# A hand-written order of tasks, rewritten from the eighth chunk on: the small product of B and C beside its neighbour's product of x and decays

## The chip, the cores and the metric

The kernel runs on one core of one Trainium2 chip. The metric is the device time of one execution in microseconds (us); the number compared is the median of several runs. Beside the runs there is one profiled execution, with a trace of every engine.

## What is computed

A scan over a sequence (a state-space layer in chunks), whose output goes through a small network that multiplies two projections:

```python
# attn: x (4, 8, 768, 32), a (4, 8, 768), B and C (4, 8, 768, 16)
cum = np.cumsum(log_a[chunk], axis=-1)
L = np.exp(cum[:, :, :, None] - cum[:, :, None, :]) * causal
CB = np.einsum('bhin,bhjn->bhij', Cc, Bc)
y_intra = np.einsum('bhij,bhjd->bhid', CB * L, xc)
y_inter = np.einsum('bhin,bhnd->bhid', Cc, state) * np.exp(cum)[..., None]
y[:, :, sl] = y_intra + y_inter
state = decay_full * state + sum_over_j(Bc * xc * decay_from_j)
# ffn: 3072 tokens, 256 -> 1024 -> 1024 -> 256
a = x @ w1; b = x @ w2
out = ((a * b) @ w3) @ w_out
```

## The kernel before

The sequence of 768 steps is cut into 16 chunks of 48 (c0 to c15). All work is written as small named tasks, and a string, PLAN, lists them in the order in which they are recorded. Each of the five queues (TensorE PE, VectorE DVE, ScalarE ACT, GpSimd POOL, and SP, which issues the DMAs) runs its own tasks in the order of that string and waits on semaphores for what another one makes. A word of the string is `task:engine@banks`: `c9.Z6:S` runs copy Z6 of chunk 9 on ACT (S; V is DVE, G is POOL), and `c9.MX@5,6` writes PSUM banks 5 and 6. For the tasks ending in `h` the number behind the @ is the slot in SBUF that holds the result. So the string fixes the order on every queue, the banks and slots, and who does each copy or sum.

The tasks of chunk c:

- `X`, `N`, `B`, `K`: loads by SP (x into `xe`, B into `bn` and `bc`, sums of logs into `ld` and `rd`). `X` fills a whole buffer `xe`, of which there are two, one for even and one for odd chunks.
- `D0`, `D1`: the exponents of the decays, one matmul each over 96 rows and 128 columns of the array (`ps<-rd,ld 96*128`). `E0`, `E1` take their exp on ACT. `W0`, `W1` (POOL) make the weighted B.
- `CB`: the product of B and C, 16 fp32 matmuls (32 records in the trace), each on 32 rows and 64 columns of the array (`ps<-bc 32*64`). `M0`, `M1` (DVE) multiply its two halves, which lie in two pairs of banks, by the decays.
- `MX`: x times the weighted decays and the old state, 32 fp32 matmuls (64 records) on 64 rows and 32 columns each (`ps<-r,xe 64*32`). It needs M, W and the state of the chunk before.
- `yi`: copies the output out of PSUM. `T` (DVE) transposes the state out of PSUM, `Z0` to `Z7` copy its eight pieces into the next chunk's `xe`, after the load `X` of that chunk. The next `MX` waits for all of them: MX, T, Z, MX is the chain from chunk to chunk.

The tasks of the network: `l<block>.<tile>.m` (two projections of a block of tokens), `a`, `g`, `h`, `l` (copy, product, rounding to fp32r and the rest); `d<block>.<tile>.m` adds one tile to the output (`ps<-fr,wo 128*128`, six matmuls), `y0`, `y1` transpose it out, `x` sends it out with 12 or 16 DMAs; `v`, `w`, `o` are weights; `s`, `x`, `q`, `t` do the last 1792 tokens with seven products in place of eight. All of these use the whole array (`128*128`).

```python
    def weigh(hf):
        w = R[:, hf * HG:(hf + 1) * HG, N:].rearrange("p (k g) s -> p k g s", k=2)
        tt("V", w, v["pc", hf], w, ALU.mult)
...
            def carry(e, q, z):
                i = z ^ (q & 1)
                copy(e, xn[64 * i:64 * i + N, q // 2, 4 * z:4 * z + 4], ZZ[32 * q:32 * q + N, 4 * z:4 * z + 4])
...
    for word in PLAN.split():
        name, _, banks = word.partition("@")
        name, _, engine = name.partition(":")
        b = [int(i) for i in banks.split(",")] if banks else []
...
            tasks.pop(name)(engine, b)
```

Of the kernel before, what the change touches and what calls it, by code (L numbers as in the profile page):

```python
# [24 lines left out]
k.act:S k.zero:V k.keep:G k.D1 t.D a.D +56x32n@0 +36x96@0 c0.B w0.D@0 k.R0:S k.L0:V t.clip:V c1.B a.clip:V t.ln:S c1.N a.ln:S c0.Y0:V k.D2 c0.N  # L25
c1.Y1:V +10x96@1 c1.X c0.Y1:V c0.X c1.Y0:V c0.D0@2 a.scan:V a.hi:V w0.L:V +10x96@3 c0.E0:S a.lo:G w0.A:S@0 c0.D1@4 w2.D@1 a.save w0.S:V c0.W0:G
c0.CB@5,6,0,1 c0.E1:S w0.H:V w1.D@2 k.S0:S c1.D1@7 c0.W1:G c0.M0:V c0.M1:V c1.D0@2 c1.E1:S w7.D@3 c2.K w0.P:V c1.W1:G c0.MX@3,4 c1.E0:S c1.W0:G
c1.CB@5,6,0,1 c0.T:V c2.X c1.M0:V c0.Z1:S c0.Z7:G +6@7 c0.Z3:S c0.Z6:G c0.Z2:S c1.M1:V c0.Z4:G c0.Z0:S c0.Z5:G c0.hi:S w6.D@0 w2.L:V w2.A:S@1 c0.lo:V
c1.MX@5,6 c1.hi:S w2.S:V c1.lo:V w2.H:S w2.P:V c1.T:V c1.Z6:G l0.0.m@1,3 c2.D1@2 c2.D0@0 w1.L:V w1.A:S@2 k.L1:S k.R1:S c2.N c1.Z2:S l0.2.m@4,7 w1.S:V
c1.Z3:S c2.B w4.D@1 c3.N c2.E0:S w7.A:S@3 w1.H:V w3.D@2 w1.P:V c2.E1:S c3.K l0.0.a:S w7.L:V l0.1.m@5,6 w6.A:S@4 w7.S:V c2.W1:G c1.Z0:S c1.Z4:S c3.X  # L30
w7.H:V l0.2.a:S c2.W0:G w5.D@3 w6.L:V w7.P:V c3.B l0.7.m@0,2 w6.S:V l0.1.a:S w6.H:S w4.A:S@0 v10.D@0 l0.0.g:V l0.1.g:V w6.P:V l0.2.g:V w4.L:V c1.Z7:S
c1.Z1:S l0.7.a:S w4.S:V c2.CB@3,4,5,6 w3.L:V l0.6.m@1,7 w4.H:S l0.7.g:V w3.A:S@1 w4.P:G c2.M1:V l0.6.a:S c2.M0:V c1.Z5:S w3.S:V c3.D0@2 c3.D1@0
c2.MX@3,4 c3.E1:S c4.K c3.E0:S c3.W1:G l0.4.m@1,5 c2.T:V c2.hi:S w5.L:V w3.H:S c5.N l0.6.g:V w5.A:S@2 o0.D@1 w3.P:G c2.lo:V c4.N l0.4.a:S w5.S:V c4.X
c2.Z0:S c3.CB@6,7,2,3 v10.A:S@3 v11.D@2 c2.Z6:G l0.3.m@0,4 c2.Z3:S c4.B c2.Z2:S c3.M1:V c2.Z4:S c3.W0:G w5.H:V c2.Z1:G l0.3.a:S c3.M0:V c2.Z7:G
c2.Z5:G l0.4.g:V c4.D1@1 c4.D0@2 w5.P:V c3.MX@5,6 c5.K l0.5.m@3,0 k.S1:S c3.hi:S c3.T:V v10.L:V c4.E1:S v13.D@3 l0.3.g:V c3.Z3:S c5.B c4.E0:S c3.lo:V
o0.A:S@4 c4.W0:G o0.L:V l1.5.m@7,1 c3.Z5:G l0.5.a:S v10.S:V c3.Z4:G l1.5.a:S l0.5.g:V o1.D@0 c4.W1:G v11.A:S@0 v11.L:V c3.Z2:G c5.D1@4 v10.H:S@0
c4.CB@5,6,2,3 c3.Z1:G c3.Z7:G c3.Z6:G l1.1.m@7,0 c4.M1:V o0.S:V l1.1.a:S v11.S:V v00.D@1 c6.B l1.5.g:V c5.D0@2 l1.4.m@3,7 c5.E0:S v12.D@2 c3.Z0:V
v13.L:V o0.H:S c5.X c4.M0:V c5.W0:G c6.K c5.E1:S o0.P:G v13.A:S@1 l1.7.m@1,2 v13.S:V v10.P:G l1.1.g:V l1.7.a:S l1.4.a:S v11.H:S@1 l1.4.g:V c4.MX@5,6
c5.W1:G l1.7.g:V v11.P:G c5.CB@0,1,3,4 c4.hi:S c6.X c4.T:V v00.A:S@2 c6.N l1.2.m@7,2 c5.M1:V v01.D@3 o1.A:S@4 v00.L:V c8.N o1.L:V v12.A:S@3 v12.L:V
v00.S:V c4.Z7:S l1.2.a:S l1.0.m@3,4 c4.lo:V c4.Z6:S v03.D@1 c4.Z4:S v13.H:S@2 c4.Z0:V c7.N l1.2.g:V o1.S:V v12.S:V c6.D0@7 c6.D1@5 c6.E0:S l1.3.m@6,2  # L40
c7.K c4.Z2:V c4.Z3:S c5.M0:V c6.W0:G l1.0.a:S c4.Z1:G c6.E1:S l1.0.g:V c4.Z5:G v00.H:S@3 c7.B c6.W1:G v13.P:V v02.D@0 l1.3.a:S c5.MX@0,1 v00.P:G
l1.3.g:V c6.CB@3,4,5,6 c5.hi:S c5.T:V c7.X v04.D@2 c5.lo:V v10.M@7,2 c5.Z6:G c6.M1:V c5.Z4:G c5.Z2:G c6.M0:V c5.Z0:G c7.D1@0 v03.L:V v12.H:S@0 c7.D0@1
v11.M o1.H:V c8.K c9.K v01.A:S@0 v01.L:V o1.P:V c5.Z5:S v03.A:S@1 l1.6.m@5,6 v12.P:V c5.Z1:V v01.S:V l1.6.a:S c5.Z3:S v02.L:V o3.D@3 c5.Z7:S v03.S:V
c7.E1:S v12.M c7.E0:S l1.6.g:V o2.D@1 v02.A:S@2 v04.L:V v01.H:V@1 c6.MX@3,4 v13.M c6.hi:S v04.A:S@4 c6.lo:V v02.S:V c6.yj:S v00.M@5,0 v04.S:V v14.D@0
c6.T:V v05.D@2 v01.P:V c6.Z5:S c6.Z4:G c8.B l2.2.m@1,6 v03.H:S@0 c6.Z0:V c6.Z6:G v02.H:S@2 o3.L:V v03.P:G o2.A:S@3 v02.P:V o3.A:S@0 l2.2.a:S c7.W0:G
v01.M v04.H:S@3 o3.S:V c6.Z7:G v14.A:S@1 o2.L:V v06.D@3 l2.5.m@3,4 c7.W1:G c8.X o2.S:V l2.2.g:V v17.D@1 v14.L:V v14.S:V l2.6.m@1,6 o2.H:V v14.H:S@1
v15.D@0 c6.Z2:V o2.P:V c10.N v05.A:S@2 c9.N v05.L:V o3.H:S c6.Z3:V c6.Z1:V l2.5.a:S o3.P:V v02.M l2.6.a:S v17.L:V v06.A:S@3 l2.6.g:V v17.A:S@0
l2.3.m@3,1 v04.P:V v17.S:V v15.A:S@4 l2.5.g:V l2.3.a:S v16.D@1 v17.H:V@2 v14.P:V v03.M v05.S:V v06.L:V v07.D@2 l2.3.g:V v14.M v05.H:S@0 v06.S:V
v16.A:S@1 v15.L:V l2.7.m@6,4 v06.H:S@1 v05.P:V v15.S:V v06.P:V v07.A:S@2 v07.L:V s0.a:V@3 v04.M v07.S:V v17.P:V v05.M v15.H:S@3 v16.L:V s0.c:G@0
l2.7.a:V v16.S:V pool.s v06.M l2.7.g:V v16.H:S@0 l2.0.m@3,1 v07.H:V@1 v16.P:V v07.P:V l2.0.a:S s0.b:V@1 s0.d:V@2 v07.M e00.a:S s0.1:V e01.a:S v15.P:V  # L50
s0.3:G l2.4.m@6,4 s0.S1h:S e00.b:V l0.0.h:S@1 e01.b:V l2.4.a:S l0.0.l:G s0.S1l:V v15.M s0.2:G l2.4.g:V l2.0.g:V c7.CB@5,6,3,4 l0.1.h:V@3 s0.S2h:S
s0.4:G c8.D0@0 c9.B c7.M1:V c8.D1@1 v16.M c8.E0:S c10.K c7.M0:V c8.E1:S s0.S2l:V c8.W0:G s0.S4h:S c8.CB@3,4,5,6 l0.2.h:S@0 c7.MX@0,1 l0.1.l:G c8.M0:V
c10.B d0.0.m@3,4 c7.yi:S c7.T:V c9.X s0.S4l:G c7.Z3:S c7.Z7:V c7.Z6:S c7.Z2:S c9.D1@0 c9.D0@1 c9.E1:S d0.1.m c11.K c7.Z5:G c7.Z4:V c9.E0:S c8.W1:G
c7.Z0:V c9.W1:G c8.M1:V l2.1.m@0,1 c9.W0:G c11.N l0.3.h:V@1 l0.4.h:S@3 c7.Z1:G c12.N l0.4.l:G l2.1.a:S s0.S3h:S l0.2.l:G s0.S3l:V c8.MX@5,6 l0.3.l:G
d0.2.m c8.yi:S c10.X l2.1.g:V c8.T:V d0.3.m l0.5.h:S@0 s1.a:V@4 c8.Z3:G c8.Z2:S c8.Z5:S c8.Z6:V c8.Z7:S c9.CB@0,1,5,6 c8.Z0:G s1.c:V@1 l0.6.h:S@1
c8.Z4:G c8.Z1:S v17.M c11.B c9.M0:V e10.a:S l0.6.l:G c9.M1:V e11.a:S e10.b:V c10.D1@0 c10.D0@1 c9.MX@5,6 l0.7.h:S@2 c12.K s1.b:V@0 c10.E1:S l0.7.l:G
# [4 lines left out]
c10.Z6:S c12.CB@0,1,5,6 l1.4.l:G l1.5.h:S@3 c10.Z3:V d0.x d1.2.m c10.Z0:S c10.Z4:S c10.Z7:S l1.5.l:G c12.M1:V d1.3.m c12.M0:V l1.6.h:S@0 s1.d:V@2
c11.MX@3,4 l1.7.h:S@1 l1.6.l:V s1.4:V l1.7.l:G d1.4.m c11.yi:S c11.T:V x0.B22h:S x0.B11l:V d1.5.m c11.Z5:S c11.Z6:S c11.Z7:G l2.0.h:S@2 c11.Z4:V
d1.6.m c11.Z0:G l2.0.l:V c11.Z1:G q0.0.P1@5 l2.1.h:V@3 l2.2.h:S@0 c11.Z3:G c13.X c11.Z2:V d1.7.m q0.0.s1:S@3 c14.B l2.1.l:V l2.2.l:V c13.D1@6
c12.MX@0,1 c13.E1:S l2.3.h:V@1 d1.y1:V c13.W1:G c13.D0@3 c12.yi:S c14.X d2.0.m@4,6 l2.3.l:G c12.T:V c13.E0:S c15.K d1.y0:V c12.Z4:S c12.Z6:S c12.Z3:V
c12.Z1:S c13.W0:G c13.CB@0,1,2,3 c12.Z5:V d1.x c12.Z7:G c13.M0:V d2.1.m c12.Z0:G c12.Z2:G c13.M1:V l2.4.h:V@2 s1.S3h:V d2.2.m l2.5.h:S@3 l2.4.l:V
s1.S3l:V c14.D1@7 l2.6.h:S@0 c13.MX@0,1 l2.5.l:V c14.E1:S l2.6.l:V c14.D0@2 c13.yi:S d2.3.m c14.W1:G c14.E0:S c13.T:V x0.B21h:V c13.Z6:S c13.Z1:G
c13.Z4:S c13.Z3:V c13.Z7:S c13.Z5:G c14.CB@0,1,2,3 c13.Z0:V l2.7.h:S@1 c13.Z2:G x0.B21l:V c14.W0:G d2.4.m c15.B c14.M1:V c14.M0:V d2.5.m l2.7.l:V
c15.X x0.T3:V@4 c14.MX@2,3 x0.B22l:V x0.T3h:V d2.6.m c14.yi:S x0.T1:V c14.T:V x0.T1h:S x0.T3l:V c15.D1@7 c14.Z7:G d2.7.m c14.Z3:S c14.Z0:S x0.T1l:V
# [787 lines left out]
```

## Time and profile before

| what | value |
|---|---|
| median of 3 runs | 264.86 us (264.73 to 265.08) |
| profiled execution | 264.53 us, span of its instructions 262.8 us |
| PE busy | 257.0 us (98%), 2870 matmul records |
| DVE, ACT, POOL busy | 205.2, 125.9, 113.2 us |
| granted TensorE clock | 1.00 |

The span runs from the first to the last instruction; the execution's own time has 1.7 us more around it. A matmul's row in the timeline gives its start and its length; matmuls overlap, so the distance from one start to the next, not the length, is what a matmul takes on PE. One row can stand for many matmuls of one kind (x12).

### The profile page before, as it was taken

Reading aid. Unit: us, or ns where it says so; the run is one execution under the profiler, and the core shown is the slowest. Engines: PE = TensorE matmul, PEld = TensorE weight load, DVE = VectorE, ACT = ScalarE, POOL = GpSimd, SP = SyncE. Lnnn points to the kernel's source line nnn. Section 1 sums busy time; section 2 is a strip of 40 time slices with the busy share of each in tenths; the row PEclk is TensorE's granted clock in tenths of the full one; section 3 lists DMA queues with packets and bytes.
Section 4 is the critical chain, followed back from the end, with each engine's and each line's share of the span. In section 5 each row is a group of like instructions: output and inputs, shape, how many; then the busy total and the mean of one; then the engine's idle time right before and its main releaser. Section 6 shows DMA issues by size and latency. Waiting matters only on the chain.

```text
span 262.8 us, 7259 instructions
## 1 busy us (share of the span) xinstructions
PE 257.0 (98%) x2870; PEld 224.9 (86%) x2870; DVE 205.2 (78%) x388; ACT 125.9 (48%) x270; POOL 113.2 (43%) x149
## 2 busy tenths in 40 slices
...
PEclk9999999999999999999999999999999999999999
...
GB/s 191 300 275 307 259 305 215 256 320 207 265 325 155 19 2 72 129 122 194 64 137 84 90 37 47 0 1 0 0 4 0 1 0 50 68 44 2 0 45 75
DMA packets 30009, 30.67 MB, mean 117 GB/s; under 512 B 15896, under 2 KB 22808, under 8 KB 29976
## 3 DMA queue, kind: packets, MB, share of 16 engines
...
q8 instruction: 22, 0.36, 0.6%
q14 instruction: 11, 0.09, 0.1%
...
## 4 chain that ended last, share of the span: by engine, by line
PE 92%; DVE 3%; issue 2%; DMA 1%; ACT 1%; DVEq 0%; ACTq 0%
PE ps L152 92%; DMA st<-in_w_dram 1%; DVE r L158 1%; DVE g L158 1%; DVE st L161 0%; DVE mag L441 0%; DVE wl L158 0%; ACT xe L164 0%; ACT mag L167 0%; DVE xT L158 0%; DVE z L363 0%; ACT r L167 0%; ACT xT L164 0%; ACT ob L164 0%; DVE zero L240 0%
## 5 line engine op out<-in xcount | busy, mean ns | idle before, releaser
L152 PE MATMUL ps<-xT,wh 128*128 128x384 f32 (+1 forms) x224 | 66.1, 363 | 0.6 <-ACT xT L164 0.6
L152 PE MATMUL ps<-fr,wo 128*128 128x384 f32 (+1 forms) x216 | 47.5, 365 | 0.0
L152 PEld LDWEIGHTS ps<-xT,wh 128*128 128x128 f32 x224 | 41.2, 188 | 5.0 <-ACT xT L164 0.7
L152 PEld LDWEIGHTS ps<-fr,wo 128*128 128x128 f32 x216 | 38.5, 188 | 4.6
L152 PE MATMUL ps<-xT,wl 128*128 128x384 f32 (+1 forms) x112 | 40.5, 362 | 0.0
L164 ACT COPY mag<-ps 128x384 f32<-128x384 f32 (+1 forms) x21 | 11.0, 526 | 35.8 <-PE ps L152 24.7
L158 POOL TENSOR_TENSOR r<-bn,r 128x128 f32<-128x128 f32 x32 | 15.8, 501 | 26.5 <-ACT r L167 9.7
L164 POOL COPY xe<-z 16x128 f32<-16x128 f32 x45 | 17.7, 393 | 21.2 <-DVE z L363 12.2
L152 PE MATMUL ps<-fr 128*128 128x256 f32 x192 | 25.2, 284 | 0.0
L152 PEld LDWEIGHTS ps<-fr 128*128 128x128 f32 x192 | 24.3, 191 | 0.8
L441 DVE SCALAR_TENSOR_TENSOR mag<-mag,st 128x512 uint32<-128x512 uint32 x28 | 21.5, 775 | 2.6 <-ACT mag L167 2.0
L158 DVE TENSOR_TENSOR mag<-ps,mag 128x384 f32<-128x384 f32 (+1 forms) x32 | 19.3, 616 | 4.6 <-PE ps L152 3.6
L152 PEld LDWEIGHTS ps<-xT,wl 128*128 128x128 f32 x112 | 21.1, 188 | 2.2 <-DVE wl L158 0.2
L164 ACT COPY g<-ps 128x384 f32<-128x384 f32 (+1 forms) x27 | 13.6, 507 | 16.6 <-PE ps L152 16.5
L167 ACT ACTIVATE mag<-st 128x512 f32<-128x512 f32 x28 | 18.7, 679 | 4.2 <-DMA st<-in_w3t_dram 2.6
L164 ACT CAST fr<-mag 128x512 fp32r<-128x512 f32 (+1 forms) x22 | 13.2, 610 | 15.0 <-PE ps L152 7.3
L158 DVE TENSOR_TENSOR r<-ps,r 128x384 f32<-128x384 f32 x32 | 16.7, 549 | 3.7 <-PE ps L152 2.2
L164 ACT COPY xe<-z 16x128 f32<-16x128 f32 x54 | 16.0, 296 | 5.4 <-DVE z L363 4.7
L158 POOL TENSOR_TENSOR fr<-mag,fr 128x512 fp32r<-128x512 f32 (+1 forms) x12 | 15.6, 1310 | 6.6 <-DVE fr L164 5.2
L167 ACT ACTIVATE r<-ps 128x384 f32<-128x384 f32 x32 | 14.9, 488 | 6.3 <-PE ps L152 6.0
L152 PE MATMUL ps<-xb,wh 128*128 128x384 f32 x64 | 16.3, 336 | 0.0
L152 PE MATMUL ps<-slot,wo 128*128 128x512 f32 (+1 forms) x72 | 15.9, 371 | 0.0
...
## 6 DMA issues: line engine op xcount, KB each, us to landing
...
```

Of the source, the lines that this page charges most:

```text
L152: pin(nc.tensor.matmul(*args, **kw))
L158: pin((nc.gpsimd if e == "G" else nc.vector).tensor_tensor(*args))
L164: pin(nc.scalar.copy(*args) if e == "S" else (nc.gpsimd if e == "G" else nc.vector).tensor_copy(*args))
L167: pin(nc.scalar.activation(*args, **kw))
L441: pin(nc.vector.scalar_tensor_tensor(m, m, 3, v["wl"].bitcast(U32), ALU.logical_shift_left, ALU.bitwise_or))
```

## The change

Only PLAN changes. It has the same 1167 words before and after: no task is added or removed. The orders on the five queues are the same up to the last matmuls of `l2.4.m`; from there the string is rewritten to its end. 152 tasks go to another engine. Banks and slots follow. Two lines of the string, of some 70:

```diff
-d0.4.m c10.E0:S c9.T:V c9.yi:S e11.b:V c11.X c9.Z7:S c10.CB@0,1,5,6 c10.W0:G x0.B11h:S l1.0.h:V@3 c10.W1:G c9.Z0:S c10.M0:V c12.B c9.Z6:S c11.D1@7
...
+c9.MX@6,7 c12.K l0.6.h:S@3 c10.W1:G c10.CB@4,5,2,3 c9.T:V l0.6.l:G c10.M0:V d0.5.m c9.Z0:S c12.B c9.yi:S c10.M1:V c11.X c9.Z4:S c9.Z2:G l0.7.h:S@1
...
```

From `c7.CB` to `c15.MX` there are nine CB and nine MX. Written in PE's order, with a bar wherever a matmul on the whole array stands between, they were `7CB | 8CB 7MX | 8MX | 9CB | 9MX | 10CB | 11CB | 10MX | 12CB | 11MX | 12MX | 13CB | 13MX | 14CB | 14MX | 15CB | 15MX` (17 groups) and are now `7CB | 8CB 7MX | 8MX | 9CB | 9MX 10CB | 11CB 10MX | 12CB 11MX | 12MX 13CB | 14CB 13MX | 15CB 14MX | 15MX` (11 groups).

PE, from `c9.MX` on. Names: `r,xe` is MX (odd chunks in `xe_96`), `bc` is CB (`bc_100` c10, `bc_101` c11), `rd,ld` the decays of c11 and then c12, `fr,wo` the tiles of `d0` and `d1`. Before:

```order
L152 MATMUL ps<-r_103,xe_96 32x64 x32
L152 MATMUL ps<-fr,wo 128x384 x6
L152 MATMUL ps<-bc_100 64x96 x16
L152 MATMUL ps<-rd_92,ld_90 128x384 x2
L152 MATMUL ps<-bc_101 64x96 x16
L152 MATMUL ps<-fr,wo 128x384 x6
L152 MATMUL ps<-r_102,xe_95 32x64 x32
L152 MATMUL ps<-rd_91,ld_89 128x384 x2
L152 MATMUL ps<-fr,wo 128x384 x24
```

Now, in the same place:

```order
L152 MATMUL ps<-r_103,xe_96 32x64 x32
L152 MATMUL ps<-bc_100 64x96 x16
L152 MATMUL ps<-fr,wo 128x384 x6
L152 MATMUL ps<-rd_92,ld_90 128x384 x2
L152 MATMUL ps<-fr,wo 128x384 x6
L152 MATMUL ps<-bc_101 64x96 x16
L152 MATMUL ps<-r_102,xe_95 32x64 x32
L152 MATMUL ps<-fr,wo 128x384 x6
L152 MATMUL ps<-rd_91,ld_89 128x384 x2
L152 MATMUL ps<-fr,wo 128x384 x12
L152 MATMUL ps<-bc_100 64x96 x16
L152 MATMUL ps<-r_103,xe_96 32x64 x32
```

The CB of c10 follows the MX of c9 at once, the CB of c11 no longer follows that of c10 behind two decays only, and between the MX of c10 and of c11 (the last row) stand three tiles of the network (18 matmuls), two decays and a CB.

ACT, from the exp of c12's decays to the copy `yi` of c11. Names: `r<-ps` is E, `fr` an `h` of the network, `xe_96` the Z of c10, `ya` a `yi`, `xT` a rounding of the last part. Before:

```order
L167 ACTIVATE r_102<-ps 128x8x48 x2
L164 CAST fr<-g_88 128x384 x2
L164 COPY xe_96<-z 16x4x32 x3
L164 CAST fr<-g_88 128x384
L164 COPY xe_96<-z 16x4x32 x3
L164 CAST fr<-g_88 128x384 x2
L164 COPY ya<-ps 128x2x192
```

Now, from the copy `yi` of c10 to that of c11:

```order
L164 COPY ya<-ps 128x2x192
L164 CAST fr<-g_88 128x384
L167 ACTIVATE r_102<-ps 128x8x48 x2
L164 CAST fr<-g_88 128x384
L164 COPY xe_96<-z 16x4x32 x3
L164 CAST xT_67<-ya 128x512
L164 COPY xe_96<-z 16x4x32
L164 CAST fr<-g_88 128x384
L164 COPY ya<-ps 128x2x192
```

The last Z of c10 on ACT stands behind both exps of c12, a rounding `fr`, three other Z and the rounding `xT`.

SP, around the output DMAs of block 0 (`out_dram<-g`, x12). Names: `xe_95` and `xe_96` are the x of c12, c13 and c14, `ld` and `rd` with 89 and 91 are the K of c14, `bn` are the N of c14 and c15, `bc_100` is the B of c14. Before:

```order
L155 DMA bc_101<-in_Ct_dram 128x640
L155 DMA bn_99<-in_Bn_dram 128x256
L155 DMA xe_95<-in_x_dram 128x512
L155 DMA ld_89<-cq 32x2x48
L155 DMA rd_91<-cq 2x16x48 x2
L155 DMA bn_97<-in_Bn_dram 128x256
L155 DMA out_dram<-g_65 32x4x64 x12
L155 DMA xe_96<-in_x_dram 128x512
L155 DMA bc_100<-in_Ct_dram 128x640
L155 DMA xe_95<-in_x_dram 128x512
```

Now:

```order
L155 DMA xe_95<-in_x_dram 128x512
L155 DMA bc_101<-in_Ct_dram 128x640
L155 DMA out_dram<-g_65 32x4x64 x12
L155 DMA bn_97<-in_Bn_dram 128x256
L155 DMA xe_96<-in_x_dram 128x512
L155 DMA ld_89<-cq 32x2x48
L155 DMA rd_91<-cq 2x16x48 x2
L155 DMA bn_99<-in_Bn_dram 128x256
L155 DMA bc_100<-in_Ct_dram 128x640
```

The K and the N of c14 and the N of c15 stand behind the twelve output DMAs now, as the x of c13 and the B of c14 did already.

## Rows read from the trace of the kernel before

**Rows 1.** The page: busy time and share of PE; its granted clock in 40 slices; the chain that ended last, by engine.

```profile
PE 257.0 (98%) x2870; PEld 224.9 (86%) x2870; DVE 205.2 (78%) x388; ACT 125.9 (48%) x270; POOL 113.2 (43%) x149
...
PEclk9999999999999999999999999999999999999999
...
PE 92%; DVE 3%; issue 2%; DMA 1%; ACT 1%; DVEq 0%; ACTq 0%
```

**Rows 2.** The chain that ended last, in order of time: start us, length us, what.

```profile
28.62 6.60 PE ps L152 x114
...
118.24 0.56 DVE r L158
...
120.69 138.59 PE ps L152 x1114
...
259.29 0.37 ACT ob L164
```

**Rows 3.** The view of waits, PE: who was waited for, us in total, times, longest.

```profile
PE ps L152 <- DVE r L158: 0.2, 1, 0.2
```

**Rows 4.** Timeline of PE in the last stage, where matmuls on the whole array follow one another: start us, length us, engine, line, operation, out<-in, rows*columns of the array, shape, count.

```profile
179.34 2.88 PE L152 MATMUL ps<-slot,wo 128*128 128x512 f32 x12
182.06 0.61 PE L152 MATMUL ps<-fr,wh 128*128 128x512 f32 x2
...
213.22 1.21 PE L152 MATMUL ps<-xb,ss 128*128 128x384 f32 x6
214.27 0.51 PE L152 MATMUL ps<-xb,wh 128*128 128x384 f32 x2
```

**Rows 5.** Timeline of PE from the decays of c8 to the MX of c10, same columns; in brackets idle time before, and what ended it.

```profile
100.63 0.62 PE L152 MATMUL ps<-rd,ld 96*128 96x384 f32 x2
101.08 1.60 PE L152 MATMUL ps<-fr 128*128 128x256 f32 x12
102.61 0.59 PE L152 MATMUL ps<-bc 32*64 32x96 f32 x32
103.13 0.86 PE L152 MATMUL ps<-r,xe 64*32 64x64 f32 x64
103.92 1.31 PE L152 MATMUL ps<-fr,wo 128*128 128x384 f32 x6
...
109.44 0.86 PE L152 MATMUL ps<-r,xe 64*32 64x64 f32 x64
110.22 2.38 PE L152 MATMUL ps<-fr,wo 128*128 128x384 f32 x12
112.53 0.59 PE L152 MATMUL ps<-bc 32*64 32x96 f32 x32
...
115.02 0.86 PE L152 MATMUL ps<-r,xe 64*32 64x64 f32 x64
115.80 1.34 PE L152 MATMUL ps<-fr,wo 128*128 128x384 f32 x6
117.07 0.59 PE L152 MATMUL ps<-bc 32*64 32x96 f32 x32
117.59 0.62 PE L152 MATMUL ps<-rd,ld 96*128 96x384 f32 x2
118.38 1.02 PE L152 MATMUL ps<-bc 32*64 32x96 f32 x32 [0.17 <-DVE r L158]
119.33 1.34 PE L152 MATMUL ps<-fr,wo 128*128 128x384 f32 x6
```

**Rows 6.** Timeline of PE, an MX with a CB directly behind it (c4 and c5), same columns.

```profile
47.77 0.86 PE L152 MATMUL ps<-r,xe 64*32 64x64 f32 x64
48.56 0.59 PE L152 MATMUL ps<-bc 32*64 32x96 f32 x32
49.08 0.44 PE L152 MATMUL ps<-xT,wh 128*128 128x384 f32 x1
```

**Rows 7.** Timeline of ACT, same columns: exp of decays, a `yi`, a rounding `h`, a rounding of 512 columns, three Z.

```profile
101.11 0.88 ACT L167 ACTIVATE r<-ps 128x384 f32<-128x384 f32 x2 [0.22 <-PE ps L152]
...
104.02 0.48 ACT L164 COPY ya<-ps 128x384 f32<-128x384 f32 x1 [1.13 <-PE ps L152]
...
113.24 0.52 ACT L164 CAST fr<-g 128x384 fp32r<-128x384 f32 x1
...
117.34 0.62 ACT L164 CAST xT<-ya 128x512 fp32r<-128x512 f32 x1
117.86 0.91 ACT L164 COPY xe<-z 16x128 f32<-16x128 f32 x3
```

**Rows 8.** Timeline of DVE, same columns: a T, the two M of a chunk, the two transposes `y0` and `y1` of a block of 384.

```profile
104.54 0.45 DVE L363 STREAM_TRANSPOSE z<-ps 128x256 f32<-128x256 f32 x1 [0.67 <-ACT ya L164]
...
117.77 1.02 DVE L158 TENSOR_TENSOR r<-ps,r 128x384 f32<-128x384 f32 x2 [0.18 <-PE ps L152]
...
250.15 1.10 DVE L565 STREAM_TRANSPOSE ob<-ps 128x384 f32<-128x384 f32 x2 [1.34 <-PE ps L152]
```

**Rows 9.** Timeline of SP: start and length of the issuing, per run of DMAs of one kind.

```profile
126.42 6.72 SPq L155 DMA_DIRECT2D out_dram<-g  x12
133.33 0.36 SPq L155 DMA_DIRECT2D xe<-in_x_dram  x1
...
137.62 6.11 SPq L155 DMA_DIRECT2D out_dram<-g  x12
```

More of the change, by code (lines that the diff above doesn't have):

```diff
@@ L24 @@
 PLAN = """
[L25 to L56, printed above, removed]
@@ L61 @@
[L61 to L68, printed above, removed]
```

98 lines of the change are left out of this document (69 added, 29 removed).

## The prediction

> **What bounds the kernel now.** I read the page first, then the chain that ended last, the waits of PE, and the timelines of PE, ACT, DVE and SP. PE is busy for 98% of the span, its clock is granted in full in every slice, and 92% of the last chain is PE [rows 1]. From 28.62 us on that chain never leaves PE but for one DVE step of 0.56 us at 118.24, and from 120.69 it is 138.59 us of PE in one piece, up to a last copy [rows 2]. The one DVE wait that the waits list for PE is that step [rows 3]. So from the place of the change on, the time is the sum of the distances between matmul starts, and a gain has to come out of that sum. The other engines matter only where PE would have to wait.
>
> Distances where only whole-array matmuls follow one another: (182.06 - 179.34) / 12 = 0.227 us for 512 columns, (214.27 - 213.22) / 6 = 0.175 for 384 [rows 4]. A CB takes 0.52 (102.61 to 103.13), an MX 0.79 (103.13 to 103.92) [rows 5].
>
> **The change part by part.**
>
> *Fewer changes of tile shape.* Between two products of small tiles, whole-array matmuls take longer than their distances say: from 110.22 to 112.53 twelve of 384 columns take 2.31, against 12 x 0.174 = 2.09, so 0.22 more; from 115.80 to 117.07 six take 1.27, against 1.05, again 0.22 [rows 5]. That price is paid per stretch between two small-tile groups, however long the stretch is. It is not paid between small tiles: the CB behind an MX starts 0.79 after it (47.77 to 48.56) and lasts 0.52 (to 49.08), the MX behind a CB lasts 0.79 [rows 5, 6], the lengths that they have alone. Whether decays stand apart or together costs nothing: a pair behind a CB takes 0.45 (100.63 to 101.08), 0.35 of it their distance and 0.1 the return from the CB, and what follows them goes on at its own distance, so they count as whole-array matmuls [rows 5]. The change takes 17 groups to 11, so six stretches vanish: 6 x 0.22 = **1.32 us**.
>
> [...]
>
> *The wait at 118 us.* Before, the CB of c11 writes the banks of the CB of c10 (0, 1, 5, 6) with two decays between, and has to wait for M0 and M1 of c10. The two decays from 117.59 last 0.79 in place of 0.35 + 0.22, the CB from 118.38 lasts 0.95 in place of 0.52, and the six matmuls from 119.33 (to the MX at 120.69) 1.36 in place of 1.27 [rows 2, 5]: 0.22 + 0.43 + 0.09 = **0.74 us**. Now d0.5, d0.6 and c11's decays stand between and the banks are others, so it goes.
>
> Without new waits the change would thus give 2.06 us.
>
> *New waits.* MX to MX is closer than before, so I walk the new order with these durations. Up to the MX of c8 (109.44) PE's rows are as before from 101.1 on. From there on each stretch is its matmuls' distances (0.174 for 384 columns, 0.227 for 512, 0.12 for 256 by the twelve from 101.08) plus 0.22, each CB 0.52, each MX 0.79. Without waits the MX of c9 then comes at 116.05, c10 at 120.5, c11 at 125.5, c12 at 131.0, c13 at 135.5.
>
> - *MX of c11.* It needs the last Z of c10 on ACT. D0 of c12 comes six matmuls after the MX of c10, at 120.5 + 0.79 + 0.11 + 6 x 0.174 = 122.45, and an exp starts 0.48 after its decay (100.63 to 101.11) [rows 5, 7]: 122.93. Then in ACT's order two exps (0.87), a rounding `h` (0.5), three Z (0.91), a rounding of 512 columns (0.52), the last Z (0.30) [rows 7]: 126.03. PE is there at 125.5: 0.55 late, or 0.35 if only the matmuls that read that piece wait (the eighth of 32 is the first). Bounds 0 (ACT's rows overlap by more) and 0.6; I take **0.45**.
> - *SP behind the outputs of d0.* They can start when `y0`, `y1` are done: d0.7 ends at 122.5, two transposes take 1.10 [rows 8], so 123.5. Twelve DMAs take 6.1 to 6.7 [rows 9], to 129.6 to 130.2; then come one load (about 0.45), the x of c13, and K of c14, issued by about 131.7. The nearest row for a landing is the end of the kernel: the last copy starts at 259.29 and lasts 0.37 [rows 2], and the span ends at 262.8, so about 3 us. An x issued at 130.4 lands near 133.4; the Z of c12, which write over it, could start at 132.9, and the MX of c13 has about half a microsecond to spare behind them. K would land near 134.7; the decays of c14 want it at 133.5 plus what was lost before (0.45). Bounds 0 (landing in 2 us) and 1.1; I take **0.3**, near the lower end, since the 3 us hold the hand-over from the last copy and the end of the program as well; that is a choice.
> - *Banks just freed.* D0 of c11 (bank 2) comes 0.1 before M1 of c10 ends: the M start 0.70 after their CB (117.07 to 117.77) and take 1.02 [rows 5, 8]; D1 of c14 is in the same position, behind the CB of c13. Bounds 0 and 0.3; I take **0.15**.
>
> Behind PE's own waits everything shifts together, and the order after `c15.MX` has the same matmuls. Walking it with the same durations I find DVE nearly full in the last 50 us but no product later than its bank. The outputs of block 2 go out much later than before, ahead of those of the last part; 16 DMAs at 0.51 (6.11 / 12) [rows 9] take 8 us there, which end before the next output is ready. Both at zero. If DVE's cover were gone, each evacuation of 384 columns would cost up to 0.55, the half of the row of two transposes [rows 8].
>
> *Sum.* -1.32 - 0.74 + 0.45 + 0.3 + 0.15 = -1.16 us. On the profiled execution: 264.53 - 1.16 = 263.4. The median of the runs lies 0.33 above it, so 264.86 - 1.16 = **263.7 us**.
>
> **The rivals.** (What a measurement of this kernel tells from no change is about 0.2%, 0.53 us.)
>
> 1. *No new waits.* The walk is too strict, ACT and SP are just in time. For it: the order before kept PE without any other wait from 28 us on [rows 2, 3]. 264.86 - 2.06 = 262.8.
> 2. *SP comes too late.* The upper bounds of the loads and of c11 hold, 1.1 + 0.6 + 0.3 = 2.0: 264.8, no change. For it: K moves behind twelve DMAs whose issue takes 6 us [rows 9]. Against it: in the old order, x issued at 133.33 behind the same DMAs [rows 9] held up nothing on PE.
> 3. *A joint costs as much as one change of shape.* Six pairs then keep half of 0.22 each and save 6 x 0.11 = 0.66: 264.86 - 0.66 - 0.74 + 0.9 = 264.4. Against it stand the rows at 48.56 and 103.13 [rows 5, 6]. That the change doesn't do what it says is this case.
> 4. *The chain MX, T, Z, MX becomes the bound: slower.* The shortest distance of two MX before is 115.02 - 109.44 = 5.58 us [rows 5]. The new order asks for 4.5 (c9 to c10), 5.0, 5.5, 4.5 (c12 to c13) and 4.4 (c14 to c15). If a chunk needed 5.58, these would fall short by 1.1 + 0.6 + 0.1 + 1.1 + 1.2 = 4.1, and the time would be 264.86 - 2.06 + 4.1 = 266.9. It decides from about 5.2 us per chunk on, where the shortfalls (0.7 + 0.2 + 0.7 + 0.8 = 2.4) pass the gain. Against it: MX to `yi` 0.89, `yi` 0.5, T 0.45, three Z 0.91 [rows 5, 7, 8] are 2.8 us; what fills the rest is other work in ACT's and DVE's queues.
>
> **How the numbers follow.** My forecast (net -0.6 to -1.7) 0.55; rival 1 0.20; rival 2 0.12; rival 3 0.05; rival 4 0.08. Faster than 264.33 are the forecast, rival 1 and half of rival 3: 0.78. Same: rival 2 and the rest of 3, 0.14. Slower: 0.08. The range reaches from rival 1 (262.8, a little below for its own spread) to rival 2 (264.8): 262.6 to 264.8. The likeliest case's own range is 263.2 to 264.3.
>
> **What would show it.** In the new timeline of PE the joined pairs start 0.79 or 0.52 after one another, and the stretch behind keeps its 0.22: then the first step holds. No wait before the CB of c11: the second. A CB or MX that lasts longer than 0.52 or 0.79, or a decay that does, marks a new wait; I look at the MX of c11 (ACT's Z), at the decays and CB of c14 (DMA), and at the Z of c12. The prediction is wrong if the joints cost 0.1 each, if the distance of two MX stays above 5 us where 4.5 is planned, or if PE waits after the MX of c15.

## The result, and the profile after

The changed kernel takes 266.87 us (median of 6 runs, 266.21 to 267.42), the kernel before beside it 264.80 (264.18 to 265.08): a ratio of 1.0079 (95% interval 1.0058 to 1.0100). It is 2.1 us **slower**; the forecast was 263.7 us, with a range of 262.6 to 264.8. The profiled execution takes 267.12 us with a span of 265.3, 2.6 more than the 264.53 of before.

The page of the changed kernel: busy time of PE, and the share of each engine in the chain that ended last [answers rows 1].

```profile
PE 257.3 (97%) x2869; PEld 225.2 (85%) x2870; DVE 204.0 (77%) x383; ACT 132.8 (50%) x287; POOL 103.3 (39%) x137
PE 80%; DMA 7%; DVE 4%; SPq 3%; issue 2%; ACT 2%; POOL 1%; DVEq 0%; POOLq 0%; ACTq 0%
```

PE does the same 257 us of work, but the last chain now leaves it for DMA, DVE, SP and ACT. The waits of PE say where: behind the start there was one of 0.2 us before [rows 3], now there are five.

```profile
PE ps L152 <- DMA bc<-in_Ct_dram: 1.4, 1, 1.4
...
PE ps L152 <- DVE g L565: 0.4, 1, 0.4
PE ps L152 <- ACT ya L164: 0.3, 1, 0.3
PE ps L152 <- DVE r L158: 0.2, 1, 0.2
PE ps L152 <- DVE xe L164: 0.2, 1, 0.2
```

The timeline of PE in order, to be read against [rows 5] (CB is `bc`, MX `r,xe`, decays `rd,ld`, `fr,wo` the tiles of d0 to d2):

```profile
104.12 1.31 PE L152 MATMUL ps<-fr,wo 128*128 128x384 f32 x6
105.68 0.62 PE L152 MATMUL ps<-rd,ld 96*128 96x384 f32 x2 [0.25 <-DVE r L158]
...
110.06 0.31 PE L152 MATMUL ps<-r,xe 64*32 64x64 f32 x6
110.62 0.81 PE L152 MATMUL ps<-r,xe 64*32 64x64 f32 x58 [0.25 <-DVE xe L164]
111.36 1.69 PE L152 MATMUL ps<-fr 128*128 128x256 f32 x12
112.89 2.25 PE L152 MATMUL ps<-fr,wo 128*128 128x384 f32 x12
115.41 0.59 PE L152 MATMUL ps<-bc 32*64 32x96 f32 x32 [0.27 <-ACT ya L164]
...
117.68 0.85 PE L152 MATMUL ps<-r,xe 64*32 64x64 f32 x64
118.46 0.59 PE L152 MATMUL ps<-bc 32*64 32x96 f32 x32
118.97 1.32 PE L152 MATMUL ps<-fr,wo 128*128 128x384 f32 x6
...
122.50 0.86 PE L152 MATMUL ps<-r,xe 64*32 64x64 f32 x64
123.29 1.33 PE L152 MATMUL ps<-fr,wo 128*128 128x384 f32 x6
124.46 0.51 PE L152 MATMUL ps<-rd,ld 96*128 96x384 f32 x2
125.34 2.35 PE L152 MATMUL ps<-fr,wo 128*128 128x384 f32 x12 [0.37 <-DVE g L565]
127.62 0.59 PE L152 MATMUL ps<-bc 32*64 32x96 f32 x32
128.14 0.86 PE L152 MATMUL ps<-r,xe 64*32 64x64 f32 x64
...
139.47 0.59 PE L152 MATMUL ps<-bc 32*64 32x96 f32 x32 [1.36 <-DMA bc<-in_Ct_dram]
```

Two things are as planned. The joined pairs cost only themselves (117.68 to 118.46 to 118.97: 0.78 and 0.51), so six stretches are gone, and the wait at 118 us is gone: 2.06 us less. What each stretch then takes beyond its matmuls and the usual 0.22 is the new part:

| where | beyond matmuls and 0.22, us | PE waits for |
|---|---|---|
| stretch from 104.12 | 0.57 (0.15 before) | a bank: decay of c9 behind M of c8, itself behind T of c7 |
| MX of c8, 110.06 | 0.51 | Z of c7 on DVE |
| stretch from 111.36 | 0.32 | `yi` of c8 on ACT (banks of CB of c9) |
| stretch from 115.93 | 0.15 | M of c9 (MX needs it, and the banks that it empties), behind two Z on DVE |
| stretches from 118.97, 128.93, pair at 121.87 | 0.25 + 0.21 + 0.11 | banks |
| stretch from 123.29 | 0.65 | `y0`, `y1` of d0: d1 takes its two banks |
| stretch from 135.17 | 1.65 | loads of c14 (1.40), a bank (0.25, which stays when the loads are early) |
| MX at 139.99, behind 152 us | 0.06 + 0.36 | small steps of 0.1 |

That is 4.7 us more than before, and -2.06 + 4.7 = +2.6, the difference of the two profiled executions. Two small things that this sum leaves out nearly cancel: PE comes to this part 0.2 us later than before (104.12 against 103.92), and a stretch of the old order (from 148.06) took some 0.1 too much as well.

Two causes can be read at once. SP issues the loads of c14 behind the 12 DMAs of d0.x; that of its `bc`, the load B, begins at 134.36:

```profile
125.37 6.40 SPq L155 DMA_DIRECT2D out_dram<-g  x12
131.87 0.38 SPq L155 DMA_DIRECT2D bn<-in_Bn_dram  x1
...
134.36 0.43 SPq L155 DMA_DIRECT2D bc<-in_Ct_dram  x1
```

And two small Z on DVE, usually 0.22 us each (the median of 13 from 100 to 156 us, in either trace), take 1.60 together, then a cast that takes 0.42 in the trace of before (at 139.59) takes 1.40:

```profile
108.96 1.60 DVE L164 COPY xe<-z 16x128 f32<-16x128 f32 x2
110.59 1.40 DVE L164 CAST wh<-mag 128x512 fp32r<-128x512 f32 x1
...
114.95 1.58 DVE L164 COPY xe<-z 16x128 f32<-16x128 f32 x2
```

Over the same time POOL runs s1.b and s1.c, two additions of 1.25 us, and beside the two Z from 114.95, which stand ahead of M of c9, it runs s1.1, a third addition that was on DVE before:

```profile
109.20 2.51 POOL L158 TENSOR_TENSOR mag<-wh,wl 128x512 f32<-128x512 f32 x2
...
115.17 1.27 POOL L158 TENSOR_TENSOR mag<-mag,mag 128x512 f32<-128x512 f32 x1
```

The second Z ends at 110.57 and the cast at 111.99, the first two additions at about 110.5 and 111.7. The chain that ended last has that Z, and the load of c14 from its issue to its landing:

```profile
109.33 1.24 DVE xe L164
...
134.36 4.98 DMA bc<-in_Ct_dram
```

### The profile page after: what moved, and what is told of

It reads as the page before. It is cut to its first block, busy times and chain, and to the rows that moved or that the text cites. A ratio compares the mean times of both kernels' runs of the same rounds, so it can differ in the third digit from the quotient of the medians.

```text
span 265.3 us, 7235 instructions
## 1 busy us (share of the span) xinstructions
PE 257.3 (97%) x2869; PEld 225.2 (85%) x2870; DVE 204.0 (77%) x383; ACT 132.8 (50%) x287; POOL 103.3 (39%) x137
## 4 chain that ended last, share of the span: by engine, by line
PE 80%; DMA 7%; DVE 4%; SPq 3%; issue 2%; ACT 2%; POOL 1%; DVEq 0%; POOLq 0%; ACTq 0%
PE ps L152 80%; SPq L155 3%; DMA bc<-in_Ct_dram 3%; DMA bc<-in_c_dram 2%; DMA cq<-cp 1%; DVE z L363 1%; ACT ya L164 1%; DVE xe L164 1%; ACT xe L164 1%; DVE r L158 1%; DVE st L161 1%; DVE g L158 1%; ACT fr L164 0%; POOL fr L158 0%; DVE mag L441 0%
## 5 line engine op out<-in xcount | busy, mean ns | idle before, releaser
L152 PE MATMUL ps<-fr,wo 128*128 128x384 f32 (+1 forms) x222 | 49.2, 364 | 0.4 <-DVE g L565 0.4
L152 PEld LDWEIGHTS ps<-fr,wo 128*128 128x128 f32 x222 | 39.6, 188 | 5.0 <-DVE g L565 0.7
L158 POOL TENSOR_TENSOR r<-bn,r 128x128 f32<-128x128 f32 x32 | 16.5, 521 | 27.0 <-ACT r L167 16.8
L164 POOL COPY xe<-z 16x128 f32<-16x128 f32 x42 | 15.8, 376 | 24.1 <-DVE z L363 13.7
L158 DVE TENSOR_TENSOR mag<-ps,mag 128x384 f32<-128x384 f32 (+1 forms) x29 | 17.4, 611 | 8.9 <-PE ps L152 6.3
L164 ACT CAST fr<-mag 128x512 fp32r<-128x512 f32 (+1 forms) x21 | 12.5, 598 | 19.5 <-DVE mag L158 7.9
L164 ACT COPY xe<-z 16x128 f32<-16x128 f32 x57 | 16.9, 296 | 8.2 <-DVE z L363 7.0
L164 ACT COPY tmp<-ps 128x512 f32<-128x512 f32 (+1 forms) x17 | 9.2, 550 | 22.6 <-PE ps L152 13.4
```

Source lines behind the costliest of these rows:

```text
L152: pin(nc.tensor.matmul(*args, **kw))
L158: pin((nc.gpsimd if e == "G" else nc.vector).tensor_tensor(*args))
L164: pin(nc.scalar.copy(*args) if e == "S" else (nc.gpsimd if e == "G" else nc.vector).tensor_copy(*args))
```

## The experiments

Each was timed beside the kernel before, whose medians were 264.76 to 264.96. The stage meant below runs from the CB of c7 to the end of the MX of c15; its length is worked out from PE's timeline (53.70 us in the changed kernel). 27 matmuls of 512 columns that lie inside it in the old order lie behind it in the new one, so only lengths of one order are compared. Diffs show words of PLAN; `...` marks what is left out.

### Parts of the change alone, on the kernel before

**e3: only the wait at 118 us.**

```diff
-c11.CB@0,1,5,6 ... d0.5.m
+d0.5.m c11.CB@0,1,5,6 ...
```

> The kernel before with the one tile d0.5 moved between the decays and the CB of c11 (and its rounding l0.5.l ahead of l1.0.h on DVE). Theory: the wait of 0.74 us at 118 us, CB of c11 for banks that the CB of c10 still holds, goes without the joining of groups, since another 1.04 us of matmuls stands there: 264.1 us against 264.8. Rival: the wait moves to the next MX or tile, because M1 of c10 sets the time there and not the banks alone: 264.8.

264.22 us, 0.9976 (0.9964 to 0.9989): 0.7 less, as expected. PE of e3, in the place of the last three of [rows 5]:

```profile
118.14 1.22 PE L152 MATMUL ps<-fr,wo 128*128 128x384 f32 x6
119.28 0.66 PE L152 MATMUL ps<-bc 32*64 32x96 f32 x32
119.88 1.32 PE L152 MATMUL ps<-fr,wo 128*128 128x384 f32 x6
```

The CB takes 0.60 in place of 0.95, and the decays ahead of it wait no more. The second term holds, and it needed no joined pair.

**e4: only one pair joined.**

```diff
-c12.CB@0,1,5,6 ... c12.M1:V ... c12.M0:V ... c11.MX@3,4 ... c11.T:V
+c12.CB@0,1,5,6 c11.MX@3,4 ... c11.T:V c12.M1:V c12.M0:V
```

> The kernel before with one group joined: the CB of c12 directly ahead of the MX of c11, M1 and M0 of c12 behind the T of c11. Theory (a stretch of matmuls on the whole array between two small groups costs 0.22 us beyond its matmuls, and joining saves that once, with nothing new to wait for): 264.6 us against 264.8, and in the trace 0.79 + 0.52 us for the pair with no gap between. Rival (joining brings a wait of its own, as M of c12 comes later on DVE): 264.9 to 265.3.

264.94 us, 1.0001 (0.9988 to 1.0013): a gain of 0.2 us lies inside the interval, and so does no gain. The trace shows the gain: from the CB of c7 to the end of the MX of c15 it takes 56.13 us against 56.32, 0.19 less, with the pair standing as forecast:

```profile
128.68 0.59 PE L152 MATMUL ps<-bc 32*64 32x96 f32 x32
129.19 0.86 PE L152 MATMUL ps<-r,xe 64*32 64x64 f32 x64
129.98 1.31 PE L152 MATMUL ps<-fr,wo 128*128 128x384 f32 x6
```

The profiled execution reached the CB of c7 0.43 us later than that of before, in a part that the edit does not touch; against such differences a gain of 0.2 is not to be seen in a time.

**e8: both.** 

> The kernel before with both single edits: d0.5 between the decays and the CB of c11, and the CB of c12 directly ahead of the MX of c11. Theory (the two are 8 us apart and add, 0.7 and 0.2 us): 264.0 us against 264.9, and both gaps closed in the trace. Rival (the M of c12 behind the T of c11 come too late now that PE is 0.7 us earlier): 264.2 to 264.5.

264.20 us, 0.9963 (0.9951 to 0.9975). It is faster than both kernels and as fast as e3. Its stage takes 55.75 us, e3's 55.67, so the second gain does not add: 0.13 us goes in the stretch from 129.44 (0.37 beyond its matmuls, 0.24 in e3), the rest in steps under 0.1, some ahead of both edits.

### The loads behind d0.x

**e1: d0.x behind the loads.** Block 1's output gets its own room, since it would otherwise wait for d0.x.

```diff
-... d0.x d1.0.m ... c15.X d1.y1:V ... d1.x
+... d1.0.m ... c15.X d1.y1:V ... d0.x d1.x
-outs(f"d{sl}.", ..., lambda: G0[:, :1024])
+outs(f"d{sl}.", ..., lambda: G1[:, :1024] if sl == 1 else G0[:, :1024])
```

> The changed kernel with one thing taken away: block 1's transposed output gets a room of its own in SBUF, and the 12 DMAs of d0.x are issued on SP behind the load X of c15 in place of ahead of the loads of c13 to c15. Theory 1 (the loads are late because SP issues 12 output DMAs first): the wait of 1.36 us of the CB of c14 for bc, 1.65 with its stretch, is gone, so about 265.3 us against 266.9 for the change; d1.x comes later and costs nothing. Rival (the load lands late whatever stands ahead of it, or the time is given back at the next MX, which waits for the Z of the chunk before): 266.5 to 267.0.

268.81 us, 1.0161 (1.0132 to 1.0189): slower still. The stage takes 52.34 us, 1.36 less, so the first half of theory 1 holds; but the part behind 152 us takes 111.3 in place of 109.3. ACT shows why:

```profile
154.75 0.62 ACT L164 CAST ss<-mag 128x512 fp32r<-128x512 f32 x1 [3.17 <-DMA out_dram<-g]
```

The last part's buffers take G1's place, and wait for the late d1.x that still reads from it. That is a fault of the room chosen, not of the order.

**e5 and e11: another room** (`YB` of the last part begins at G0's word 1536, block 1's output is in words 768 to 1535). **e10** has the room alone; **e12** and **e13** are single profiled executions of e5's kernel.

> As the run before with d0.x behind c15.X, but the room for block 1's transposed output is now in the buffer of block 0's products (768 words of it, the last part's second x moved up by 512 words), not in one that is given to the last part's buffers at 152 us. Theory (the first room made those buffers wait for the late d1.x, which cost 2.0 us behind 152 us, and the load of c14 is late by SP alone): no wait for the load, no wait behind 152 us, 265.5 us against 266.9 for the change. Rival (the late d1.x holds up something else, or the 1.4 us are given back at a later wait): 266.5 or more.

> The control of the run with the second room: the changed kernel with block 1's transposed output in the buffer of block 0's products and the last part's second x moved up by 512 words, but with d0.x where the change has it. Theory 1 (a place in SBUF costs nothing): as the change, 266.9 us. Theory 2 (the place costs something, by which the run with d0.x behind c15.X lost what it gained): 267.4 or more.

> The run with the second room and d0.x behind c15.X once more, beside its control on the same chip. Theory 1 (the load of c14 is worth the 1.4 us that its stage shows, and the profiled execution started late by chance): 0.9 to 1.4 us under the control. Theory 2 (most of it is lost again): 0.3 us under the control, or nothing.

> One more profiled execution of the kernel with the second room and d0.x behind c15.X, to see where an execution of 266.5 us loses what one of 265.5 us does not. Theory 1: in the loads and decays ahead of 27 us, as in the first of its profiled executions. Theory 2: behind 152 us. Theory 3: at a wait between 100 and 152 us that the two profiled ones do not show.

> A third look at the same kernel, with the same three theories: the loss ahead of 27 us, between 100 and 152 us, or behind 152 us.

| run | time, us | profiled | to the CB of c7 | stage | rest to the last matmul |
|---|---|---|---|---|---|
| the change | 266.87 | 267.12 | 98.87 | 53.70 | 109.30 |
| e10, room alone | 266.41 | 266.53 | 98.56 | 53.43 | 109.30 |
| e5 | 266.56 | 266.64 | 99.67 | 52.29 | 109.46 |
| e11 | 266.60 | 265.51 | 98.48 | 52.33 | 109.47 |
| e12 | one execution | 265.73 | 98.69 | 52.35 | 109.47 |
| e13 | one execution | 266.21 | 98.91 | 52.60 | 109.49 |

In all four traces with d0.x behind the loads the stage is 1.1 to 1.4 us shorter than in the change, and PE has no wait for a DMA there. In e11 SP issues the load at 130.89, and on PE (second view) the CB of c14 follows its decay without a wait:

```profile
130.89 0.43 SPq L155 DMA_DIRECT2D bc<-in_Ct_dram  x1
```

```profile
137.40 0.34 PE L152 MATMUL ps<-rd,ld 96*128 96x384 f32 x1
137.70 0.59 PE L152 MATMUL ps<-bc 32*64 32x96 f32 x32
```

0.16 to 0.19 is given back behind 152 us. The medians show less: e5 and e11 lie 0.3 under the change, and not under e10, the control of e11, which shows that the new room alone costs nothing. Part of what is missing is the time to the CB of c7, which the edit does not touch and which ranges from 98.48 to 99.67. Of the theories on where an execution loses it, the first fits e5, which comes 0.8 us later than the change to the CB of c7. e12 and e13 lost little anywhere (0.25 in one stretch of e13) and were short, so they do not show what a long execution loses. How much of the 1.1 to 1.4 us a run without a trace gains stays open.

**e14: the 12 DMAs left out. e15: 20 in place of 12.**

```diff
-for g in range(NR4):
+for g in range(0 if n == "d0." else NR4):              # e14
+for g in [0, 1, 2, 0, 1] if n == "d0." else range(NR4): # e15
```

> The changed kernel without the 12 DMAs that send block 0's output out (d0.x; that part of the output is left out). Nothing else moves. Theory 1 (these 12 stand ahead of the loads of c14 on SP, and the wait of the CB of c14 costs 1.1 to 1.4 us in an ordinary execution): 265.4 to 265.8 us against 266.4 to 266.9, and no wait of PE for a DMA behind 100 us. Theory 2 (what the load costs in its stage is given back at a later wait, whatever takes it away): 266.4 or more, with a new wait of PE behind 140 us. Theory 3 (no new wait, but executions without the 12 DMAs start late as often): the median near 266.5 and single executions at 265.5.

> The changed kernel with 20 DMAs in place of 12 in d0.x: two of its three groups of rows are sent out twice, the same data to the same place. SP is held 8 x 0.53 = 4.2 us longer at that place. Theory 1 (in ordinary executions the loads behind d0.x already hold up PE, as in the profiled one): the whole 4.2 us come on top, 270.7 to 271.1 us. Theory 2 (in ordinary executions the loads have some slack, and only the profiled ones were late): 4.2 less that slack, 269.5 to 270.2 for a slack of about 1 us. Theory 3 (the loads' place on SP doesn't matter): 266.9.

e14: 266.11 us (265.46 to 267.05). Its stage takes 52.37 us, with no wait for a DMA and no new one of size; the profiled execution came late, at 99.76, to the CB of c7. The median is 0.8 under the change, between theory 1 (265.4 to 265.8) and theory 3 (near 266.5); no new wait and a late start are what theory 3 says.

e15: 271.91 us (271.31 to 273.40), 5.0 over the change where its 8 more DMAs hold SP 4.1 us longer (10.48 in place of 6.40). SP, then PE, then the view of a window, whose columns behind the five engines are the granted clock, the share of the DMA engines and GB/s:

```profile
126.31 10.48 SPq L155 DMA_DIRECT2D out_dram<-g  x20
```

```profile
141.17 0.42 PE L152 MATMUL ps<-rd,ld 96*128 96x384 f32 x1 [3.67 <-DMA rd<-cq]
143.40 0.94 PE L152 MATMUL ps<-bc 32*64 32x96 f32 x32
```

```profile
142.00:145.00 3.00, 3.00 (x90) 2.34 (x93) 1.64 (x4) 2.23 (x6) 1.11 (x3) 0.50 0.68 210
```

The decay of c14 waits 3.67 us for K. Behind that wait the granted clock is 0.50 from 142 to 145 us, and from this decay to the end of the MX of c13 PE needs 4.19 us (141.17 to 145.36), against 3.04 in e14 (137.35 to 140.39): 1.15 more, taken here as the slower clock's. The stage is 3.5 us longer than in the change: about 3.67 + 1.15, less the change's 1.40. The place of the loads on SP matters, so theory 3 falls. Theories 1 and 2 are not told apart: all six runs have a mean clock of 0.985 to 0.994 (0.998 to 1.00 in the change), and what they would take at the full clock is not known.

How long an ordinary execution of the change waits for these loads therefore stays open. Worked out as the 1.40 was, the profiled executions of e10 and of e2 (below), with d0.x in the same place, lose 1.14 and 0.6. The load B itself is not always equally long: from issue to landing it takes 4.98 us in the change, 5.23 in e6, 4.08 in e9 and 3.77 in e10, under 3.4 in e2 (issued at 134.87, used at 138.21 without a wait) and under 3.8 in e15 (139.69, 143.40). So it is late by its place behind d0.x and by a long transfer together; what makes the transfer long was not followed.

### Copies on DVE beside POOL, and `yi`

**e2: s1.b and s1.c on DVE.**

```diff
-s1.b:G@4 ... s1.c:G@2
+s1.b:V@4 s1.c:V@2
```

> The changed kernel with the two sums s1.b and s1.c on DVE instead of POOL. Theory 1 (a small copy from SBUF to SBUF on DVE stands still while POOL adds, so that the Z of c7 and c8 on DVE end 1 us late): the DVE copies of 109 to 115 us take 0.2 instead of 1.2 us, the MX of c8 does not wait in its middle (0.51 us) and the CB of c9 does not wait (0.3 us), so 0.5 to 0.8 us less than the change, about 266.2 us. Rival (DVE is full there, and 1 us more of sums on it holds up T and M): 266.9 to 267.5, with waits of PE for DVE where the others were. A third outcome: the copies on DVE are as slow without POOL beside them, and then nothing of the 0.8 us goes.

DVE of e2, the same two Z and the same cast:

```profile
108.91 0.58 DVE L164 COPY xe<-z 16x128 f32<-16x128 f32 x2
109.88 0.43 DVE L164 CAST wh<-mag 128x512 fp32r<-128x512 f32 x1 [0.39 <-PE ps L152]
```

0.58 in place of 1.60 and 0.43 in place of 1.40: the third outcome falls, and the cause is shown. The two Z beside s1.1, which stays on POOL, take 1.58 us here too. The MX of c8 takes 0.79 again. But the kernel takes 267.13 us, 1.0071 (1.0045 to 1.0098), no less. At 134.69, behind the CB of c13, the profiled execution of e2 is 0.48 us ahead of that of the change (0.42 from an equal start), and at the CB of c14 1.26 us (138.21 against 139.47). It loses this again to new waits of PE: 0.58 us for `rd<-cq` ahead of the decay at 136.59, 0.35 for DVE at 139.94, and 0.43 at 142.39. The rival is right on the time, though not by a full DVE alone.

**e6: `yi` of c8 ahead of its Z on ACT** (`c8.Z6:S c8.Z0:S c8.yi:S` becomes `c8.yi:S c8.Z6:S c8.Z0:S`).

> The changed kernel with the copy yi of c8 ahead of the copies Z6 and Z0 of c8 on ACT. Theory (the CB of c9 writes banks 4 and 5 of the MX of c8, and waits 0.3 us for the last of their two readers, yi): the wait goes, 266.6 us. Rival (the Z, 0.45 us later, hold up the MX of c9 by as much): 266.9.

267.32 us, 1.0087 (1.0053 to 1.0122), no gain. The CB of c9 waits no more; the MX of c9 does, with the decay ahead of it, for DVE:

```profile
114.75 0.59 PE L152 MATMUL ps<-bc 32*64 32x96 f32 x32
...
117.52 0.85 PE L152 MATMUL ps<-r,xe 64*32 64x64 f32 x64 [0.22 <-DVE r L158]
```

CB to MX is 2.77 us, and 2.27 in the change. The 0.34 us is more than given back 2 us later.

**e7: e5, e2 and e6 together.** 

> The changed kernel with the three cures together: d0.x behind c15.X with a room of its own for block 1's output, s1.b and s1.c on DVE, yi of c8 ahead of Z6. Theory (the three waits are apart from each other and each is worth what it was read for, 1.4, 0.45 and 0.3 us): 264.8 us, no more than the kernel before, since the small waits for banks stay. Rival (they give back to a common chain, MX, T, Z, MX, from 104 to 140 us): 265.5 to 266.

266.50 us, 1.0057 (1.0032 to 1.0082). Its stage is 52.05 us, 1.65 less than the change's, of the 2.15 that the sum of the parts would be. Two waits of 0.56 and 0.43 us at 83 and 95 us, ahead of the stage, fell into its profiled execution; its runs reach from 265.17 to 268.97. None of the cures brings this order to the kernel before.

### The wait at 124 us: banks, or the chain

**e9: d0.7 ahead of the CB of c11.** **e16: besides, its transposes ahead of T, a decay behind d1.0.**

```diff
-c11.CB@2,3,4,5 ... c10.MX@6,7 l1.0.l:G d0.7.m c10.yi:S c10.T:V ... d0.y0:V ... d0.y1:V c12.D0@2 c12.D1@7 ... d1.0.m@1,0
+d0.7.m c11.CB@2,3,4,5 ... c10.MX@6,7 l1.0.l:G d0.y0:V d0.y1:V c10.yi:S c10.T:V ... c12.D0@2 ... d1.0.m@1,0 c12.D1@7
```

(e16; e9 moves `d0.7.m` alone.)

> The changed kernel with one tile, d0.7, moved on PE from behind the MX of c10 to ahead of the CB of c11, directly behind d0.6. Every other queue is as it was. Theory 1 (the 0.4 to 0.65 us at 123 to 125 us are a wait for banks alone: d1.0 takes over the two banks of d0, which the two transposes of d0 must empty first): the transposes run beside CB and MX, d1.0 waits no more, 266.4 us against 266.9. Theory 2 (that wait only hides another, the chain MX, T, Z, MX: the last Z of c10 on ACT ends 4.7 us behind the MX of c10, and the matmuls between the two MX are cut to some 3.2 us): the MX of c11 waits 1 to 1.5 us for ACT, and the kernel takes 267.4 to 267.9.

> As the run with d0.7 ahead of the CB of c11, and now the two transposes of d0 also stand ahead of the T of c10 on DVE, and one of c12's two decays behind d1.0 on PE, so that neither d1.0 nor a decay has to wait for DVE behind the MX of c10. Theory 1 (the wait at 124 us is for banks alone): d1.0 starts some 0.6 us behind the end of the MX of c10 in place of 2.05, the MX of c11 without a wait; with the matmuls gone from between, the MX of c11 comes 3.6 us behind that end, and the kernel takes 266.0 to 266.4 us. Theory 2 (MX, T, Z, MX is nearly as long there: the last Z of c10 ends 4.5 us behind the MX): the CB of c12 runs early, then the MX of c11 waits about 0.8 us for the Z on ACT, and the kernel takes 266.8 to 267.3 us, no better than the change.

e9: 267.95 us, 1.0136 (1.0107 to 1.0165). Its time is that of theory 2, its reason is neither's: d1.0 still waits for the transposes, which stand behind T on DVE, and T behind `yi` (PE, then DVE).

```profile
126.32 2.38 PE L152 MATMUL ps<-fr,wo 128*128 128x384 f32 x12 [0.49 <-DVE g L565]
```

```profile
124.89 0.45 DVE L363 STREAM_TRANSPOSE z<-ps 128x256 f32<-128x256 f32 x1 [0.67 <-ACT ya L164]
125.26 1.00 DVE L565 STREAM_TRANSPOSE g<-ps 128x384 f32<-128x384 f32 x2
```

d1.0 comes 2.04 us behind the end of the MX of c10 (124.28), as in the change (123.29 to 125.34), with or without six matmuls between. The stage of the profiled execution is only 0.3 us longer than the change's; four of the six runs have a mean clock of 0.992 to 0.994, and the two at 0.999 and 1.00 take 267.45 and 267.62. e16: 267.31 us, 1.0083 (1.0054 to 1.0113), no better than the change. The wait for the banks is gone; now d1.0 waits for its rounding on ACT and the MX of c11 for the last Z there (PE, then ACT):

```profile
125.06 1.30 PE L152 MATMUL ps<-fr,wo 128*128 128x384 f32 x6 [0.60 <-ACT fr L164]
...
128.21 0.90 PE L152 MATMUL ps<-r,xe 64*32 64x64 f32 x14
129.49 0.74 PE L152 MATMUL ps<-r,xe 64*32 64x64 f32 x50 [0.38 <-ACT xe L164]
130.16 1.14 PE L152 MATMUL ps<-fr,wo 128*128 128x384 f32 x5
```

```profile
129.15 0.29 ACT L164 COPY xe<-z 16x128 f32<-16x128 f32 x1
```

So theory 2: banks and chain are of nearly one length there, and curing the first shows the second. One thing more: here PE is 1.2 us later than in the change at the end of that MX (130.16 against 128.93), yet its CB of c14 comes at 139.31, not later than 139.47. The load was there. In e9 PE is 1.0 us later than in the change at 129.94, and 0.36 at the CB of c14. So a wait for a late load hides what PE loses ahead of it. That a gain ahead of it would be worth nothing follows, but is not shown: e6 gave its gain back before, and in e2 the load came in time.

## Why the prediction was wrong

- **Six stretches, -1.32: right, by PE's rows.** Four of the six joined pairs cost themselves alone, the other two 0.11 and 0.06 more; the 0.11 is a bank that the exp of c11's decay empties until 122.44. e4's trace gives 0.19 for one pair; all six were not measured by themselves. Rival 3 falls: four of its joints show nothing of its 0.11. Where CB and MX touch, the rows hold their own 0.52 and 0.79; a stretch of matmuls on the whole array between two groups of small tiles holds 0.22 beyond its distances, and what makes that up no run shows.
- **The wait at 118 us, -0.74: right.** e3 measures 0.7.
- **"Up to the MX of c8 PE's rows are as before", and no wait from there to the MX of c9: wrong, 1.4 us.** PE's order there is nearly the same, but banks and engines are not. The decays of c9 have the banks of the CB of c8, which M of c8 empties only behind T of c7, and before they had those that T itself emptied (0.42 more from 104.12). s1.b and s1.c moved to POOL, where they hold up Z of c7 (0.51) and, through T and `yi`, the CB of c9 (0.32); s1.1 moved too and holds up M of c9 (0.15). The walk took PE's rows and ACT's durations, and no DVE copy's duration beside POOL's work; without two of these additions two Z take 0.58 in place of 1.60 (e2).
- **MX of c11, +0.45: size near (0.65) by luck, reason wrong.** The MX comes at once; two tiles ahead of it, d1.0 waits for the banks of d0, which the walk left out. e16 shows the Z on ACT close behind, as forecast.
- **SP behind d0.x, +0.3 (0 to 1.1): place right, size wrong.** It is 1.40 in the profiled execution of the change, 1.14 and 0.6 in those of e10 and e2; for ordinary executions it stays open. Three things were mis-sized. d0.x starts at 125.37, not 123.5, as its transposes stand behind T. The load that PE waits for in the change is B of c14, behind K and two N on SP, which the walk did not time. And it takes 4.98 us from issue to landing, against the 3 reckoned, of which the prediction chose the low end because they held the program's end too.
- **Banks just freed, +0.15 (0 to 0.3): mis-sized.** 0.57 in three places, and 0.25 in the stretch with the decays of c14.
- **Behind the MX of c15, 0: nearly right.** 0.36 more, in steps of 0.1 that were not followed further.
- **Rival 4** gave the right sign and 266.9, but by luck: its mechanism does not hold. Two MX can follow at 4.82 us (117.68 to 122.50) and at 4.41 (147.37 to 151.78), so no chunk needs 5.58. What is right in it is that from c10 to c11 MX, `yi`, T, Z, MX leaves hardly any room (e16). The chance of 0.08 for a slower kernel was too low: the walk counted only the new waits that it found, each by itself. The order before had been clear of waits, and the new one asks for everything earlier.
